# A chunked recurrence with two gated layers: the fills, the first keys and the first units of the start in another order

## The chip, the core and the metric

The kernel runs on one core of a Trainium2 chip. The metric is device time in microseconds (us), the median of several runs of one launch. The engines are named as in the profile: PE is TensorE's matrix multiply, PEld its weight load, DVE VectorE, ACT ScalarE, POOL GpSimd, SP the engine that issues the DMAs.

## The reference

Three layers follow one another. The first is a recurrence over 768 steps for 4 x 8 independent heads, with a state of 40 x 40:

```python
for t in range(S):
    y[:, :, t] = np.einsum('bhd,bhde->bhe', rt, state)
    Sa = np.einsum('bhde,bhe->bhd', state, at)
    state = state * wt[:, :, None, :] - np.einsum('bhd,bhe->bhde', Sa, bt) + np.einsum('bhd,bhe->bhde', vt, kt)
```

Its output, 3072 rows of 320, goes through `silu(x @ w_gate) * (x @ w_val) @ w_out` with 1536 hidden columns, and through a second such layer with `sigmoid` in place of `silu`. All data is float32.

## The kernel before, in words

**Chunks.** The 768 steps are cut into 12 chunks of 64. Inside a chunk the recurrence becomes matrix products and the inverse of one triangular 64 x 64 matrix per head pair (16 of them, `NS`). For each chunk `m` four generators do the work:

- `prep_a(m)` (line 435) scales the inputs a, b, k by running products of w, transposes them on PE (`tr4`, line 352) and forms the products `kps` ("keys", line 471). ACT negates them into `bn` (lines 480, 481), DVE masks them into `lq` (line 483).
- `prep_b(m)` (line 607) inverts. For chunks 0 to 2 `halves` (line 531) solves 16 x 16 blocks on DVE and joins them on PE; for the others `whole` (line 495) solves 32 x 32 blocks. Two more products, `zps` and `xps`, finish the inverse X; its last step is line 654 on ACT.
- `chain(m)` (line 657) carries the state `sT` from chunk to chunk: it copies the state into `Q` (line 667), transposes it into `sd` (lines 669, 670), and forms `qps`, `ups` (which needs X) and `sps`, for two halves of the heads. All three share one PSUM bank.
- `post(m)` (line 725) forms the chunk's outputs `ysb` (line 777).

**The running products of w.** Chunks 0 to 3 get them by a scan on DVE (line 138): chunk 0 in `first` (line 174), chunks 1 to 3 in `scanned` (line 388). The scan tiles of chunks 1 to 3 have the tags `raw3`, `raw4`, `raw5`, and the tile `one` that all scans read has the tag `raw2`. Chunks 4 to 11 get them from `powers(1)` and `powers(2)` (line 218): DVE clamps w (line 231), POOL multiplies (line 228, 29 products of 128 x 320 for a group), and the results go to DRAM (line 258) through two big tiles with the tags `wt` and `wq`.

**The gated layers.** `extra(m)` (line 1196) runs the first gated layer for the 128 x 2 rows of chunk `m`, with the weights loaded so far: `split` (transposes and a high and low part), then for each weight block 16 gate products (`gate`, line 976, tile `gv`) and 6 sums (`add`, line 994), which use the PSUM tags `po0` and `po1`. `extra(-2)` loads the first three weight blocks, `extra(0)` its own units and then blocks four and five. A weight block is loaded in three pieces (`load_w`, line 855): each goes from DRAM into a `raw` tile, through ACT (line 874), POOL (line 875), DVE (lines 878 to 884), ACT (line 894, the first write into the weight tile) and POOL (lines 896 to 902). The first three blocks use the tags `raw` and `raw1` by turns; from `extra(0)` on, all six from `raw` to `raw5` in turn, the fourth block beginning at `raw3`. Blocks four and five are stored in the tiles `wt` and `wq`, once `powers(2)` has let them go. The rest of the first layer and the second follow as one long stream on PE from about 700 us on.

**What sets the order.** Every loop step puts its generators into `merge` (line 790) with an interval and an offset, and `merge` emits the one whose next part is due first. The order of emission is a priority: a planner with a cost model of its own then places the instructions on each engine, and one that was emitted later can stand earlier where it is ready sooner. `behind` (line 111) pins an instruction behind a marked one of the same engine. Tiles with one tag share their memory, so a new one waits for every access to the one before. Each engine runs its list in order.

**Parts that the change touches.** `static` (line 58) collects the tiles that start as zero in `fills`; `fill` (line 80) lets ACT copy a zero into them. It is called at line 266 for `lq0` and at line 816, after `prep_a(0)`, for the other twelve. The marks are "keys" (the last product of `first` into `tkb`, line 199, for the first clamp of `powers(1)`), and "joined" and "merged" (the last products of chunk 0 at lines 586 and 642), behind which the first and third group of chunk 1's key transposes are pinned (line 465). `first` opens a PSUM pool of its own, whose banks go over to the pools of `banks()` afterwards; the two banks of `ptp`, which all transposes use, come first in it.

The start of the main loop reads:

```python
merge([(prep_a(0), 1, 0)])
fill()
...
merge(start)                     # prep_b(0) and prep_a(1)
for m in range(NCH + 1):         # cp(m), prep_b(m + 1), prep_a(m + 2), ahead(m) = extra(m - 1)
```

## Time and profile before

| | us |
|---|---|
| median of three runs | 1339.35 |
| lowest and highest of them | 1336.72, 1343.93 |
| the profiled execution | 1336.38 |
| its span, first to last instruction | 1334.6 |
| busy in it: PE, PEld, DVE, ACT, POOL | 1239.4, 1179.4, 754.5, 599.3, 563.1 |

All the times of the trace are of the profiled execution and count from the start of its span. A row of a timeline gives start and duration in us, engine, line, operation, the tile written and the one read, the shape, and in brackets the idle time of the engine just before it and what ended that. PEclk is the granted TensorE clock as a share of full speed. Chunk `m` is known by its place in the list of a line: the third L539 is that of chunk 2.

### The profile page before, as it was taken

What the parts mean: (1) busy time and instruction counts of PE and PEld (TensorE: products, weight loads), DVE (VectorE), ACT (ScalarE), POOL (GpSimd) and SP (SyncE); (2) the same over time, 40 slices, a digit from 0 to 9 for tenths busy, and PEclk for the clock granted to TensorE, in tenths of its full rate; (3) what the DMA queues carried; (4) which work ended last, traced back from release to release, by engine and by line L of the source; (5) the groups of instructions that cost most, each with busy time, mean ns of one, the idle gap of its engine ahead of it and who ended that gap; (6) DMA issues with size and microseconds to landing.
All of it is one profiled execution on the core that took longest, in us unless ns stands there. A gap on an engine that the chain in (4) does not pass through costs nothing.

```text
span 1334.6 us, 34566 instructions
## 1 busy us (share of the span) xinstructions
PE 1239.4 (93%) x14209; PEld 1179.4 (88%) x14209; DVE 754.5 (57%) x1578; ACT 599.3 (45%) x1446; POOL 563.1 (42%) x767
## 2 busy tenths in 40 slices
PE   5486889999999999989899999999999999999996
PEld 4475788898899888988898999999999999999995
DVE  6858667876687668775879888733122122211221
ACT  8353664556655565545444444423333333333331
POOL 5658241222322222445777888833222222222221
PEclk7667696999999999989999999999999999999998
DMA  7545823535533443253355555321000000000000
GB/s 211 125 123 131 191 91 103 124 98 129 144 92 99 129 123 90 70 139 102 118 172 179 190 167 165 97 81 56 23 23 23 23 23 23 23 23 23 11 11 14
DMA packets 153065, 126.16 MB, mean 95 GB/s; under 512 B 100928, under 2 KB 131136, under 8 KB 152640
## 3 DMA queue, kind: packets, MB, share of 16 engines
q1 hardware_dynamic: 152896, 123.84, 33.0%
q8 instruction: 114, 1.87, 0.6%
q14 instruction: 55, 0.45, 0.1%
HBM read 92.05 MB, written 31.76 MB: 93 GB/s over the span
## 4 chain that ended last, share of the span: by engine, by line
PE 75%; DVE 12%; issue 3%; ACT 3%; DMA 2%; POOL 2%; SPq 1%; POOLq 0%; DVEq 0%; ACTq 0%
PE g L976 30%; PE po L994 18%; PE gv L976 9%; PE tp L356 3%; PE kps L471 3%; PE aps L741 2%; PE yps L767 2%; PE qps L677 1%; PE ups L695 1%; SPq L258 1%; DVE dt L879 1%; DVE pr L511 1%; DVE part L517 1%; PE zps L626 1%; PE xps L642 1%
## 5 line engine op out<-in xcount | busy, mean ns | idle before, releaser
L976 PE MATMUL g<-x,w 128*128 128x256 f32 x3520 | 491.2, 283 | 4.1 <-DVE g L982 2.3
L976 PEld LDWEIGHTS g<-x,w 128*128 128x128 f32 x3520 | 460.5, 190 | 5.9 <-DVE g L982 3.2
L985 POOL TENSOR_TENSOR hl<-g,hh 128x256 fp32r<-128x256 f32 x288 | 218.9, 761 | 482.7 <-ACT hh L984 435.9
L983 DVE TENSOR_TENSOR g<-g,g 128x256 f32<-128x256 f32 x220 | 93.0, 423 | 308.7 <-PE g L976 299.1
L984 ACT CAST hh<-g 128x256 fp32r<-128x256 f32 x288 | 117.0, 406 | 259.7 <-DVE g L983 234.0
L994 PE MATMUL po<-w,hh 128*128 128x320 f32 x1152 | 225.3, 311 | 0.9 <-ACT hh L984 0.8
L994 PEld LDWEIGHTS po<-w,hh 128*128 128x128 f32 x1152 | 175.4, 189 | 2.2 <-ACT hh L984 1.7
L976 PE MATMUL gv<-x,w 128*128 128x256 f32 x1088 | 160.0, 296 | 5.9 <-ACT x L928 3.6
L976 PEld LDWEIGHTS gv<-x,w 128*128 128x128 f32 x1088 | 142.0, 197 | 11.9 <-ACT x L928 6.0
L980 ACT ACTIVATE g<-g 128x256 f32<-128x256 f32 x220 | 84.4, 384 | 132.4 <-PE g L976 120.7
L994 PE MATMUL po<-w,hl 128*128 128x320 f32 x576 | 141.9, 316 | 0.5 <-POOL hl L985 0.5
L896 POOL TENSOR_TENSOR dt<-dt,w 128x384 f32<-128x384 f32 (+1 forms) x72 | 78.5, 1091 | 72.4 <-ACT w L894 37.5
L994 PEld LDWEIGHTS po<-w,hl 128*128 128x128 f32 x576 | 91.9, 190 | 1.8 <-POOL hl L985 1.0
L483 DVE TENSOR_TENSOR lq<-kps,part 64x256 f32<-64x256 f32 x96 | 40.4, 421 | 86.5 <-ACT bn L481 82.8
L511 DVE TENSOR_TENSOR pr<-part,sn 128x4 f32<-128x4 f32 (+4 forms) x135 | 74.2, 550 | 2.9
L741 PE MATMUL aps<-rbd,ut 104*128 104x128 f32 x384 | 58.2, 295 | 14.1 <-DVE am L749 5.6
L517 DVE TENSOR_REDUCE part<-pr 128x2 f32<-128x4 f32 (+4 forms) x135 | 66.7, 494 | 3.1
L471 PE MATMUL kps<-lq,kbt 104*128 104x128 f32 x384 | 64.4, 320 | 3.4 <-ACT kbt L467 1.8
L356 PE MATMUL tp<-ident,part 128*104 128x128 f32 x288 | 50.0, 301 | 16.2 <-ACT pend L168 6.3
L741 PEld LDWEIGHTS aps<-rbd,ut 104*128 104x128 f32 x384 | 51.3, 203 | 15.6 <-issue 8.6
L471 PEld LDWEIGHTS kps<-lq,kbt 104*128 104x128 f32 x384 | 56.6, 226 | 7.2 <-issue 3.7
L894 ACT CAST w<-dt 128x384 fp32r<-128x384 f32 (+1 forms) x72 | 35.6, 494 | 57.1 <-DVE dt L879 49.1
(171 smaller groups left out, 1758.1 us busy)
## 6 DMA issues: line engine op xcount, KB each, us to landing
raw<-in_w_dram SPq DMA_DIRECT2D x48, 384.0 KB
xd<-x SPq DMA_DIRECT2D x12, 896.0 KB
x<-xd SPq DMA_DIRECT2D x12, 896.0 KB
raw<-in_w_dram SPq DMA_DIRECT2D x24, 320.0 KB
ld<-in_a_kb_dram SPq DMA_DIRECT2D x22, 320.0 KB
ld<-rd SPq DMA_DIRECT2D x32, 160.0 KB
pn<-pd SPq DMA_DIRECT2D x32, 160.0 KB
ld<-in_a_a_dram SPq DMA_DIRECT2D x12, 320.0 KB
```

The costliest lines, as they stand in the source:

```text
L356: t = nc.tensor.transpose(ps[0 : x.shape[1], n, :], x, ident)
L471: nc.tensor.matmul(kps[:, n].rearrange("p h t -> p (h t)"), lhsT=kbt[0:PW, n, :], rhs=lq[m % 3][0:PW, 4 * g4 + n].rearrange("p h t -> p (h ...
L511: nc.vector.tensor_tensor(out=o, in0=xs[:, 0:kk, None, 0:n].to_broadcast([P, kk, 2, n]), in1=sn[:, None, n : n + 2, 0:n].to_broadcast([P, ...
L517: nc.vector.tensor_reduce(out=xs[:, 0:kk, n : n + 2], in_=o, axis=AX.X, op=ALU.add)
L741: nc.tensor.matmul(aps[:, n, h2], lhsT=ut[0:PW, x, 2 * h2 : 2 * h2 + 2].rearrange("p u s -> p (u s)"), rhs=rbd[0:PW, x, h2].rearrange("p b ...
L896: sub(out=tf, in0=tf, in1=w.bitcast(F32), op=ALU.subtract)
L976: nc.tensor.matmul(gv[n], lhsT=p, rhs=q, start=e == 0, stop=e == len(seq) - 1)
L980: nc.scalar.activation(out=g, in_=gv[0], func=AF.Sigmoid)
L983: nc.vector.tensor_tensor(out=g, in0=gv[1], in1=g, op=ALU.mult)
L984: nc.scalar.copy(out=hh, in_=g)
L985: self.heng.tensor_tensor(out=hl, in0=g, in1=hh.bitcast(F32), op=ALU.subtract)
L994: self.nc.tensor.matmul(ops[u], lhsT=p[:, us], rhs=q, start=first and n == 0, stop=last and n == 2)
```

## The change

1. `fills` becomes a table by name. Five tiles (`lq0`, `qv`, `lq1`, `sT`, `x16`) are filled before `prep_a(0)`; the other eight after it, each pinned on ACT behind the mark "keys", which is now the last negation of the keys (line 481) emitted so far.
2. `first` puts a dummy tile over the first two banks of its PSUM pool, so that its own tiles lie in others. The small product and copy that make chunk 0's pending scale (lines 166 to 168) move from the end of `first` behind the transposes of `an` in `prep_a(0)`, into a tile of `ptp`. The banks of chunk 0's third and fourth key group change places.
3. Both clamps of `powers(1)` are pinned behind the last scaling of chunk 0's solve (line 569) instead of the first one behind the first keys.
4. The marks "joined" and "merged" go, and chunk 1's keys use three banks by turns instead of one.
5. In `halves` the sign scaling (line 540) and the diagonal (line 546) go from ACT to DVE.
6. For chunk 0 `chain` leaves out the copies of the state and its transposes, as the state is zero.
7. `extra(0)` is emitted at the end of loop step 0 instead of within step 1, ahead of `prep_a(3)` and `prep_b(2)`.

The diff without its plain renamings:

```diff
-    def fill():
-        for t in fills:
-            nc.scalar.copy(out=t, in_=zero[(slice(None),) + (None,) * (len(t.shape) - 2)].to_broadcast(t.shape))
-        fills.clear()
+    def fill(ts, mark=None):
+        for t in ts:
+            to = nc.scalar.copy(out=t, in_=zero[(slice(None),) + (None,) * (len(t.shape) - 2)].to_broadcast(t.shape))
+            if mark:
+                behind(to, mark)
...
-                marks.pop(name).ins.name,
+                marks[name].ins.name,
...
+            pp.tile([P, 2, 512], F32, tag="f", name="f")
             ps = [pp.tile([P, 10, 64 * i + 64], F32, tag=f"f{i}", name=f"f{i}") for i in range(2)]
...
-            pt = pp.tile([P, NS], F32, tag="f2", name="f2")
...
-            ends_scan(0, p, pt)
+            end_rows(p)
...
-            behind(clamp, "keys")
+            if n == 1:
+                behind(clamp, ("solved", 0))
...
-    lq = [static([P, NS, 2, C], "lq0", 0.0)]
-    fill()
+    lq = [static([P, NS, 2, C], f"lq{i}", 0.0) for i in range(3)]
...
-    fills.append(x16)
-    lq += [static([P, NS, 2, C], f"lq{i}") for i in (1, 2)]
     xinv = [static([P, NS, C], f"xinv{i}", part="part1") for i in range(2)]
-    fills.extend(lq[1:])
+    early = ("lq0", "qv", "lq1", "sT")
+    fill([fills[n] for n in early] + [x16])
...
+        if m == 0:
+            ends_scan(0, ptp.tile([P, 4, P], F32, tag="tp", name="pep")[:, 0, 0:NS])
...
-            ps = tr4(lambda n: tk[:, 4 * g4 + n], ("joined", None, "merged", None)[g4] if m == 1 else None)
+            ps = tr4(lambda n: tk[:, 4 * g4 + n])
...
-            pool, tag = ((pmm, "mm"), (pzy, "zy"), (pqu, "qu"), (po, "po1"))[g4 if m == 0 else 0]
+            pool, tag = ((pmm, "mm"), (pzy, "zy"), (po, "po1"), (pqu, "qu"))[g4 if m == 0 else g4 % 3 if m == 1 else 0]
...
-                nc.scalar.mul(out=bn[hi, q, 0:32], in_=kps[hi, :, h2, 32:64], mul=-1.0)
+                marks["keys"] = nc.scalar.mul(out=bn[hi, q, 0:32], in_=kps[hi, :, h2, 32:64], mul=-1.0)
...
-        nc.scalar.mul(out=sn, in_=full[:, :, 0:16], mul=par[:, 0:1])
+        nc.vector.tensor_scalar(out=sn, in0=full[:, :, 0:16], scalar1=par[:, 0:1], scalar2=None, op0=ALU.mult)
...
-        nc.scalar.mul(out=x16.rearrange("p r t -> p (r t)")[:, 1:256:34], in_=nk, mul=-1.0)
+        nc.vector.tensor_scalar(
+            out=x16.rearrange("p r t -> p (r t)")[:, 1:256:34], in0=nk, scalar1=-1.0, scalar2=None, op0=ALU.mult
+        )
...
-            nc.vector.tensor_scalar(out=to(0), in0=src, scalar1=sel[:, z : z + 1], scalar2=None, op0=ALU.mult)
+            marks[("solved", m)] = nc.vector.tensor_scalar(out=to(0), in0=src, scalar1=sel[:, z : z + 1], scalar2=None, op0=ALU.mult)
...
-        if m == 0:
-            marks["joined"] = last
...
-        if m == 0:
-            marks["merged"] = last
...
-            for h2 in range(2):
-                nc.scalar.copy(out=two(Q[E40[h2], h2, sg]), in_=pairs(sT, s4)[E40[h2]])
-
-            ps = tr4(lambda n: sT[:, 4 * hb + n])
-            nc.scalar.copy(
-                out=sd[0:PW, s4], in_=ps[0:PW].rearrange("p n (h e) -> p n h e", h=2)[..., 0:D]
-            )
+            if m:
+                for h2 in range(2):
+                    nc.scalar.copy(out=two(Q[E40[h2], h2, sg]), in_=pairs(sT, s4)[E40[h2]])
+
+                ps = tr4(lambda n: sT[:, 4 * hb + n])
+                nc.scalar.copy(
+                    out=sd[0:PW, s4], in_=ps[0:PW].rearrange("p n (h e) -> p n h e", h=2)[..., 0:D]
+                )
...
-    fill()
+    fill([t for n, t in fills.items() if n not in early], "keys")
...
-        todo.append((ahead(m), *(NX if m > 0 else QX)))
+        if m == 0:
+            todo.append((extra(0, out), 0.05, 3))
+        if m > 1:
+            todo.append((ahead(m), *NX))
```

## Rows read from the trace of the kernel before

**Rows 1.** The page: the chain of waits that ended last, by engine.
```profile
PE 75%; DVE 12%; issue 3%; ACT 3%; DMA 2%; POOL 2%; SPq 1%; POOLq 0%; DVEq 0%; ACTq 0%
```

**Rows 2.** Busy time by stretch: PE, PEld, DVE, ACT, POOL busy, PEclk, DMA share, GB/s.
```profile
0.00:40.00 40.00, 24.49 (x252) 21.86 (x252) 27.67 (x58) 31.50 (x54) 23.82 (x41) 0.79 0.64 176
40.00:60.00 20.00, 4.07 (x136) 3.13 (x136) 19.55 (x41) 6.38 (x13) 14.20 (x19) 0.54 0.68 156
60.00:160.00 100.00, 76.26 (x1359) 66.92 (x1360) 64.25 (x130) 47.32 (x110) 55.60 (x68) 0.67 0.65 145
160.00:260.00 100.00, 94.52 (x1494) 86.53 (x1494) 74.02 (x154) 55.24 (x131) 32.79 (x47) 0.82 0.37 108
```

**Rows 3.** Timeline of PE, 0 to 20 us: start, duration, line, tile, [idle before].
```profile
6.91 2.40 PE L153 MATMUL f<-ident,bn 128*64 128x64 f32 x40 [6.91 <-DVE bn L138]
...
18.82 1.95 PE L356 MATMUL tp<-ident,part 128*104 128x128 f32 x8 [6.27 <-ACT pend L168]
```

**Rows 4.** ACT: the fills' line (ns min/median/max, first and last start), then its timeline.
```profile
L82 ACT COPY part<-part x7: 534/719/1252, 3.9 to 11.6; 128x640 f32<-128x640 f32 x2, 128x416 f32<-128x416 f32 x2, 128x1280 f32<-128x1280 f32 x1, 128x832 f32<-128x832 f32 x1
L82 ACT COPY lq<-part x3: 1892/1892/1897, 2.1 to 14.2; 128x2048 f32<-128x2048 f32 x3
...
16.10 1.87 ACT L667 COPY part<-part 40x320 f32<-40x320 f32 x4
18.00 0.69 ACT L203 COPY pn<-f 128x640 f32<-128x640 f32 x1
```

**Rows 5.** Timelines of DVE and PE, 44 to 85 us: chunk 1's inputs and keys.
```profile
44.95 0.45 DVE L410 TENSOR_TENSOR tkb<-ld,dtp 128x128 f32<-128x128 f32 x2
...
55.51 1.90 PE L573 MATMUL hps<-x1t,bn 16*32 16x16 f32 x128 [8.89 <-DVE x1t L563]
...
61.42 1.95 PE L356 MATMUL tp<-ident,tkb 128*104 128x128 f32 x8
...
83.81 1.16 PE L471 MATMUL kps<-lq,kbt 104*128 104x128 f32 x8
```

**Rows 6.** Timeline of ACT: the last step of the inverses of chunks 0, 1, 3.
```profile
71.80 1.20 ACT L654 ACTIVATE part<-xps 32x512 f32<-32x512 f32 x2
...
149.63 1.20 ACT L654 ACTIVATE part<-xps 32x512 f32<-32x512 f32 x2
...
255.48 1.19 ACT L654 ACTIVATE part<-xps 32x512 f32<-32x512 f32 x2 [0.84 <-PE xps L642]
```

**Rows 7.** DVE: first and last step of two solves; products of L552 in each.
```profile
37.86 1.08 DVE L539 STREAM_TRANSPOSE sn<-bn 128x512 f32<-128x512 f32 x1
...
56.58 1.23 DVE L569 TENSOR_SCALAR part<-pr,part 128x256 f32<-128x256 f32 x2
...
149.98 1.02 DVE L539 STREAM_TRANSPOSE sn<-bn 128x512 f32<-128x512 f32 x1
...
161.92 1.76 DVE L569 TENSOR_SCALAR part<-pr,part 128x256 f32<-128x256 f32 x2
...
L552 DVE TENSOR_TENSOR pr<-x,sn x7: 297/625/1215, 45.9 to 52.9; 128x8 f32<-128x8 f32 x1, 128x32 f32<-128x32 f32 x1, 128x72 f32<-128x72 f32 x1, 128x128 f32<-128x128 f32 x1
...
L552 DVE TENSOR_TENSOR pr<-x,sn x7: 168/291/562, 153.1 to 157.8; 128x8 f32<-128x8 f32 x1, 128x32 f32<-128x32 f32 x1, 128x72 f32<-128x72 f32 x1, 128x128 f32<-128x128 f32 x1
```

**Rows 8.** Powers on POOL (10 to 80 us), chunk 0's scan, fourth weight's first write.
```profile
L228 POOL TENSOR_TENSOR wp<-wp x14: 849/864/2162, 17.4 to 52.6; 128x320 f32<-128x320 f32 x14
...
7.05 1.63 DVE L138 TENSOR_TENSOR_SCAN pr<-sn,one 128x264 f32<-128x264 f32 x3
...
139.20 0.51 ACT L894 CAST w<-dt 128x384 fp32r<-128x384 f32 x1 [3.67 <-issue]
```

**Rows 9.** Busy time of line 976 alone: PE, PEld, PEclk, DMA share, GB/s.
```profile
158.00:187.00 29.00, 8.45 (x48) 7.54 (x48) 0.83 0.37 118
```

**Rows 10.** Timelines of DVE and ACT: chunk 4's long solve and inverse.
```profile
238.51 1.23 DVE L497 STREAM_TRANSPOSE sn<-bn 128x1024 f32<-128x1024 f32 x1
...
296.97 1.19 ACT L654 ACTIVATE part<-xps 32x512 f32<-32x512 f32 x2 [1.92 <-PE xps L642]
```

More of the change, by code (lines that the diff above doesn't have):

```diff
@@ L53, in attention @@
     dr = ctx.enter_context(tc.tile_pool(name="at_dram", bufs=2, space=DRAM))
-    room, fills = {}, []
+    room, fills = {}, {}
     def static(shape, name, val=None, part=None):
@@ L74, in static @@
         if val == 0.0:
-            fills.append(t)
+            fills[name] = t
         elif val is not None:
@@ L157, in load_w0, with end_rows @@
         nc.sync.dma_start(out=x[:, :, 1 : C + 1], in_=w0[m].rearrange("p (j t) -> p j t", t=C))
-    def ends_scan(m, p, ps):
+    def end_rows(p):
         nc.vector.tensor_tensor(
@@ L165, in ends_scan @@
         )
+    def ends_scan(m, ps):
         nc.tensor.matmul(ps[0:PW], lhsT=pe[:, 0], rhs=hot, start=True, stop=True)
@@ L198, in first @@
                 sl = slice(8 * n, 8 * n + 8)
-                marks["keys"] = nc.vector.tensor_tensor(
+                nc.vector.tensor_tensor(
                     out=pairs(tkb[0], sl), in0=heads(xk)[:, sl], in1=ipv[:, sl], op=ALU.mult
@@ L350, in loads_late, with tr4 @@
             dma(out=ut[e, :, 1:3].rearrange("d n h t -> d n (h t)"), in_=vt[m, b2].rearrange("d (n t) -> d n t", t=P))
-    def tr4(get, name=None):
+    def tr4(get):
         ps = ptp.tile([P, 4, P], F32, tag="tp", name="tp")
@@ L355, in tr4 @@
             x = get(n)
-            t = nc.tensor.transpose(ps[0 : x.shape[1], n, :], x, ident)
-            if n == 0 and name:
-                behind(t, name)
+            nc.tensor.transpose(ps[0 : x.shape[1], n, :], x, ident)
         return ps
@@ L428, in scanned @@
                     turn(ps[:, 256 + 64 * i : 320 + 64 * i], p[:, 8 + i, 0:C], True)
-                ends_scan(m, p, ps[:, 384:400])
+                end_rows(p)
+                ends_scan(m, ps[:, 384:400])
                 by_p(ps[:, 256:384], slice(32, 40))
@@ L585, in halves @@
                 at = 32 * (j % 2) + 16
-                last = nc.tensor.matmul(
+                nc.tensor.matmul(
                     ps[32 * j : 32 * j + 16, q, 16:32],
@@ L641, in prep_b @@
                 lo, hi = slice(64 * h2, 64 * h2 + 32), slice(64 * h2 + 32, 64 * h2 + 64)
-                last = nc.tensor.matmul(
+                nc.tensor.matmul(
                     ps[lo, q],
```

## The prediction

> **What bounds the kernel now.** I read the chain of waits first. It gives TensorE three quarters of the span and VectorE an eighth [rows 1], so the end of the kernel moves only if TensorE gets its work earlier or has less of it. The busy time by stretch says where that can be [rows 2]. TensorE is busy for 94.5 of the 100 us from 160 to 260. Before 160 it is busy for 24.5 + 4.1 + 76.3 = 105 us, and most of that at a granted clock of 0.54 to 0.79. Weighted by the clock, the first 160 us hold 24.5 x 0.79 + 4.1 x 0.54 + 76.3 x 0.67 = 73 us of full-speed work, so 87 us are lost there. The next 100 us lose 100 - 94.5 x 0.82 = 22. Every part of the change lies in this start, so I looked for what TensorE waits for in it.
>
> There are three such places. From 12.6 to 18.8 it waits for ScalarE [rows 3]: the first transposes need a PSUM bank that `first` still holds. The row names the copy of the pending scale (L168), which stands right behind the copy that empties this bank (L203); L203 was ready at 9.3, when the transposes into it end [rows 3], but stands at 18.0 behind the fills and the copies of the zero state [rows 4]. From 46.6 to 55.5 it waits for VectorE, which solves chunk 0's triangular systems [rows 5], although the keys of chunk 1 were nearly ready: their transposes are pinned behind two marks of chunk 0 and start at 61.4, and the last product ends at 85.0 [rows 5]. And the inverse of each early chunk comes just in time or late: X is complete at 73.0, 150.8 and, for chunk 3, 256.7 [rows 6]; the chain of that chunk cannot start its second product earlier.
>
> **The change, part by part.**
>
> *Fills.* ScalarE's fills and zero-state copies run from 2.1 to 18.0 [rows 4]. With only five fills in front, two of 1.9 us and three of 0.4 to 1.25 [rows 4], some 6 us after the table load, the copy at L203 can run when its input is there, and the two PSUM banks put aside in `first` free the transposes of it. They then wait only for their own input and for the second scan's transposes. I take the whole wait, 6 us [rows 3]; the ends are 0 (the planner finds other work for ScalarE) and 9 (18.0 - 9.3). The eight late fills, three of 1.9 us and five of 0.5 to 0.6, still cost some 8 us on ScalarE after the first keys; the solve of chunk 0, which no longer uses ScalarE, covers them. Without that cover they would hold up chunk 1's copies by as much.
>
> *Clamps behind the solve, two ScalarE steps on VectorE.* The power products on GpSimd started at 17.4 [rows 8], behind a clamp on VectorE; now both clamps of the first group wait for chunk 0's solve. The solve took from 37.9 to 57.8, 20 us, with GpSimd multiplying beside it. Chunk 2's, with GpSimd idle for most of it, took 150.0 to 163.7, 13.7 us [rows 7]. The seven products of the solve show why: median 625 ns in the first case, 291 in the second [rows 7]. I take 7 us off the solve; the ends are 2 (weight conversion keeps GpSimd busy) and 9. The sign scaling and the diagonal move from ScalarE to VectorE: the nearest rows on VectorE, two pairs of scalings of 128x256, take 1.23 and 1.76 us a pair [rows 7], 0.6 to 0.9 each, about what a step and the hand-over to ScalarE take. So this is between 1 us gained and 1 us lost per chunk, and I count it in the 7.
> The Trainium skill (SBUF — State Buffer, Who interferes with whom) says that a VectorE instruction with two SBUF inputs, or one in a two-port mode, and a reading GpSimd instruction shut each other out. By that rule the contention is not removed but moves to chunk 1's solve, and the sum below would be 12 instead of 19, or 1327; the trace agrees with the rule on the products [rows 7]. I don't take it off: GpSimd was busy for 56 of the 100 us in which chunk 1's solve ran before [rows 2], so that solve paid already.
>
> *Keys of chunk 1.* Without the marks they may fill the 8.9 us gap [rows 5]. With three banks in place of one, a product no longer waits until the one before is read out. They need chunk 1's scaled inputs, ready at 45.4 [rows 5], so I put their end at about 68 instead of 85.
>
> *The zero state.* Four ScalarE copies of 0.46 us [rows 4], two more and eight transposes go: 3 us of TensorE and ScalarE at most, hidden in gaps. I give it nothing.
>
> *First units with chunk 0.* The 48 gate products and their sums move from 158 to 187, where TensorE is full, to the gaps before 150; the gate products alone are 8.5 us [rows 9]. They need chunk 1's inverse only for a PSUM bank.
>
> Together: the inverse of chunk 0 at about 57 (16 us earlier: 6 + 7, and 3 for the interleaved transposes), that of chunk 1 at about 105 instead of 151 (keys end at 68, then a solve and its five short products, as long as chunk 0's 73.0 - 37.9 = 35 us [rows 6, 7]). Chunks 0 to 2 and the first units are then through some 30 to 45 us earlier than before.
>
> **What is late next.** This does not all reach the end. Two power groups still have to run before the fourth and fifth weights can be written, as these use the same two tiles. And since the first units are now emitted with chunk 0, the pieces of the fourth weight claim the three raw tiles before the scan of chunk 3 does, which uses the same ones. So chunk 3's scan waits for the weight, and the weight for the second power group. Before, the first write of the fourth weight was released at 139.2 [rows 8]. The first product moves from 17.4 to about 47, behind a solve that ends near 45, which shifts this by 30 if all is rigid: 169. But GpSimd needed 36 us from the first to the last of 14 products of 0.86 us [rows 8], because the other products and the weight conversion stood between; with most of the conversion done before, 15 to 30 us of the shift come back. I take 150, ends 137 and 169. From there: 15 us for three pieces, then scan to inverse. For chunk 0 that was 8.7 to 73.0, 64 us [rows 6, 8]; chunk 3 has the long solve, which in chunk 4 took 59.7 us against 35, at low priority [rows 6, 10], so 0 to 25 more, and I take 12. The inverse of chunk 3 comes at 150 + 15 + 64 + 12 = 241, against 256.7: 16 us earlier (ends: 216, 41 earlier; 273, 16 later). TensorE has the second units and later keys to do in the meantime; I count 3 us for work it gets out of the way. **Sum: -19 us** on the profiled execution, whose own time is 1336.4 with a span of 1334.6. That is 1317; the median of the three runs is 3 above that execution, so I say 1320.
>
> **Rivals.** *The wait swallows it (19%).* If the fourth weight is released after about 160, chunk 3's inverse lands within 6 us of where it was, and the early gain is spent in TensorE waiting between chunks 2 and 3: 1333 to 1345. This also covers a planner that puts the new order back much as it was. For it: the planner's placing by priority, and a VectorE busy for 74 of 100 us from 160 to 260 [rows 2]. Against it: work that TensorE did meanwhile stays done.
> *Slower: the raw tiles (15%).* If all of the 30 us shift stays and the long solve takes its full 60, chunk 3's inverse comes at 169 + 15 + 64 + 25 = 273, 16 us late, and each later chunk is solved behind it: 1339 + 16 - 3 = 1352. The point from which it decides is a release after 169. For it: both power groups are serial through one pair of tiles, with a load and two stores between. Against it: GpSimd is idle for 44 of the 100 us from 60 to 160 [rows 2], room for the second group.
> *The clock follows (10%, inside the faster share).* The granted clock was 0.54 from 40 to 60, while TensorE was busy for a fifth of the time, and 0.67 in the 100 us after [rows 2]. With the gaps filled, the 76 us of work there could go at the upper level, 2.4 GHz, from the beginning: 76 x (1 - 0.67) = 25 us less, of which chunk 3's wait leaves perhaps half; 1320 - 13 = 1307. The Trainium skill (TensorE: Matmul & The Clock Gate, What's actually happening) says that the throttled state is the default and that activity releases it; by that rule this case is the expected one. I give it no more, since TensorE was busy for three quarters of that stretch and still had 0.67 [rows 2].
>
> **How the numbers follow.** The forecast, a gain of 8 to 30 us, has 56%; with the clock's 10% that is 0.66 for faster by over 0.5% (6.7 us, about what a measurement of this kernel can tell from no change). The swallowed gain has 19%, slower 15%. The range goes from 1339 - 41 = 1298, the early end of chunk 3's inverse, to 1345, the end of the swallowed case; of the slower case most lies outside.
>
> **What would show it.** First transposes at 12 to 14 with no wait on the copy for the pending scale; chunk 0's solve under 15 us; keys of chunk 1 in the gap at 45 to 65; the first gate products before 130 instead of 158.9; the fourth weight's first write near 150, and chunk 3's scan behind it. The forecast is wrong if chunk 1's inverse is not before 125, or if chunk 3's is not before 250.

## The result and the profile after

The changed kernel takes 1347.62 us (median of 14 runs, 1344.01 to 1350.24), the kernel before 1339.28 beside it: a ratio of 1.006, 95% interval [1.0047, 1.0073]. It is 8.3 us slower, where 19 us faster was predicted. The rival "slower: the raw tiles", with its 1352, comes near it.

The chain of waits of the changed kernel, by engine, stands against [rows 1]:

```profile
PE 68%; DVE 15%; DMA 5%; ACT 5%; issue 3%; POOL 3%; SPq 1%; DVEq 0%; POOLq 0%; ACTq 0%
```

TensorE's share of the chain falls from 75% to 68%, and other engines and transfers take it. The busy time by stretch says where (columns and stretches as in [rows 2]):

```profile
0.00:40.00 40.00, 25.14 (x252) 22.40 (x252) 24.93 (x60) 25.56 (x43) 10.72 (x30) 0.79 0.55 170
40.00:60.00 20.00, 11.69 (x296) 9.45 (x296) 17.68 (x41) 12.29 (x25) 9.63 (x10) 0.65 0.52 156
60.00:160.00 100.00, 71.53 (x1156) 62.53 (x1156) 66.10 (x124) 42.76 (x97) 67.66 (x88) 0.66 0.52 123
160.00:260.00 100.00, 79.12 (x1226) 70.95 (x1228) 64.31 (x135) 48.32 (x116) 30.37 (x38) 0.76 0.42 117
```

Weighted by the clock, TensorE does 25.14 x 0.79 + 11.69 x 0.65 + 71.53 x 0.66 = 75 us of full-speed work before 160, 2 more than before. From 160 to 260 it does 79.12 x 0.76 = 60, where it did 94.52 x 0.82 = 78 [rows 2]. So the start gained next to nothing, and 17 us went in the stretch that had been nearly full; the kernel is 8.3 us longer in the end.

What TensorE waits for in that stretch (timelines of ACT, DVE and PE, rows in order of time):

```profile
157.14 0.51 ACT L899 CAST w<-dt 128x384 fp32r<-128x384 f32 x1 [2.03 <-DMA pd<-wp]
...
165.10 2.13 DVE L139 TENSOR_TENSOR_SCAN s<-s,one 128x660 f32<-128x660 f32 x1
167.29 1.97 PE L154 MATMUL dtp<-ident,s 128*64 128x64 f32 x32 [3.71 <-DVE s L139]
171.72 2.00 DVE L139 TENSOR_TENSOR_SCAN s<-s,one 128x660 f32<-128x660 f32 x1
173.77 4.96 PE L154 MATMUL dtp<-ident,s 128*64 128x128 f32 x48 [4.52 <-DVE s L139]
186.15 0.55 DVE L719 TENSOR_TENSOR part<-part,pend 104x320 f32<-104x320 f32 x1
```

The first row is the first write of the fourth weight, 139.2 before [rows 8]; it waited for the store of the second power group (`pd`). Then chunk 3's two scans, and TensorE waits for them twice. The last row completes the first half of chunk 1's state. The same two scans, the state, and the last step of chunk 2's inverse in the kernel before:

```profile
115.23 1.58 DVE L138 TENSOR_TENSOR_SCAN s<-s,one 128x660 f32<-128x660 f32 x1
120.60 2.00 DVE L138 TENSOR_TENSOR_SCAN s<-s,one 128x660 f32<-128x660 f32 x1
...
166.15 0.49 DVE L717 TENSOR_TENSOR part<-part,pend 104x320 f32<-104x320 f32 x1
...
212.78 1.20 ACT L654 ACTIVATE part<-xps 32x512 f32<-32x512 f32 x2 [1.27 <-PE xps L642]
```

The scans come 50 us later than before, and the state 20.

The inverses of chunks 0 to 3 (ACT, last step, as in [rows 6]):

```profile
71.86 1.20 ACT L655 ACTIVATE part<-xps 32x512 f32<-32x512 f32 x2
...
139.55 1.20 ACT L655 ACTIVATE part<-xps 32x512 f32<-32x512 f32 x2
...
226.32 1.20 ACT L655 ACTIVATE part<-xps 32x512 f32<-32x512 f32 x2 [1.27 <-PE xps L645]
...
271.58 1.18 ACT L655 ACTIVATE part<-xps 32x512 f32<-32x512 f32 x2
```

Chunk 0's stayed where it was, chunk 1's came 10 us earlier, chunk 2's 14 and chunk 3's 16 later. The step from chunk 1's to chunk 2's grew from 63 to 87 us: there the gain turned into the loss.

### The profile page after: what moved, and what is told of

Read it like the earlier page. It is cut to its first block, busy times and chain, and to the rows that moved or that the text cites. A ratio compares the mean times of both kernels' runs of the same rounds, so it can differ in the third digit from the quotient of the medians.

```text
span 1347.7 us, 34551 instructions
## 1 busy us (share of the span) xinstructions
PE 1242.2 (92%) x14201; PEld 1177.9 (87%) x14201; DVE 759.4 (56%) x1584; ACT 594.5 (44%) x1434; POOL 559.7 (42%) x767
## 4 chain that ended last, share of the span: by engine, by line
PE 68%; DVE 15%; DMA 5%; ACT 5%; issue 3%; POOL 3%; SPq 1%; DVEq 0%; POOLq 0%; ACTq 0%
PE g L981 26%; PE po L999 16%; PE gv L981 8%; PE tp L358 3%; PE aps L743 3%; PE kps L474 2%; PE yps L769 2%; PE qps L679 2%; DVE dt L884 1%; DVE ds L889 1%; DVE pr L514 1%; PE ups L697 1%; DVE part L520 1%; DMA wt<-in_a_w_dram 1%; DVE g L987 1%
## 5 line engine op out<-in xcount | busy, mean ns | idle before, releaser
L889 DVE SCALAR_TENSOR_TENSOR ds<-raw,ds 128x384 f32<-128x384 uint32 (+1 forms) x72 | 60.0, 833 | 1.2
```

## Experiments

Eighteen kernels were timed against the kernel before, each beside runs of its own of that kernel. The medians can differ from the ratios by some tenths of a per cent, so effects are given by the ratios, in points (1 point is 1%, 13.4 us). The times of the inverses and of chunk 3's first scan (us) are the starts of these steps in one trace of each.

| kernel | us | ratio and 95% interval | inverse of 1, 2, 3 | scan of 3 |
|---|---|---|---|---|
| before | 1339.28 | | 150, 213, 255 | 115 |
| changed | 1347.62 | 1.006 [1.0047, 1.0073] | 140, 226, 272 | 165 |
| A: without 7 | 1335.69 | 1.0003 [0.9979, 1.0027] | 149, 211, 256 | 110 |
| B: loads late | 1333.08 | 0.9969 [0.9949, 0.9989] | 151, 215, 260 | 113 |
| C: without 3 | 1351.7 | 1.0113 [1.0092, 1.0133] | 161, 228, 271 | 143 |
| D: 7 alone | 1332.67 | 0.9967 [0.9944, 0.999] | 136, 204, 247 | 147 |
| E: without 3, 7 | 1326.1 | 0.9892 [0.9859, 0.9924] | 136, 204, 249 | 111 |
| F: B, pieces held | 1334.98 | 0.998 [0.995, 1.0009] | 148, 214, 255 | 121 |
| G: keys of 3 later | 1352.46 | 1.0102 [1.008, 1.0125] | 138, 214, 265 | 166 |
| H: B, keys of 2 later | 1349.82 | 1.0077 [1.0051, 1.0104] | 131, 225, 270 | 129 |
| I: B without 3 | 1338.1 | 0.9982 [0.995, 1.0013] | 139, 205, 251 | 113 |
| J: E without 4 | 1344.46 | 1.0044 [1.0021, 1.0067] | 161, 225, 268 | 122 |
| K: E without 1, 2 | 1344.88 | 1.0043 [1.0023, 1.0063] | 139, 211, 256 | 120 |
| L: E without 5 | 1331.39 | 0.9942 [0.9922, 0.9962] | 138, 204, 249 | 121 |
| M: A, second clamps later | 1329.23 | 0.9928 [0.9907, 0.995] | 140, 205, 253 | 113 |
| N: changed, two raw tiles | 1335.67 | 0.9996 [0.997, 1.0023] | 137, 204, 250 | 117 |
| O: E, pieces held | 1341.98 | 1.0034 [1.0013, 1.0055] | 155, 218, 259 | 123 |
| P: C, two raw tiles | 1321.49 | 0.9865 [0.9832, 0.9897] | 138, 203, 249 | 112 |
| Q: changed, M's and N's edits | 1327.4 | 0.9926 [0.9898, 0.9954] | 138, 211, 256 | 114 |
| R: D, two raw tiles | 1336.88 | 0.9994 [0.9974, 1.0015] | 150, 218, 265 | 115 |

### Undoing parts 7 and 3 (A to D)

A puts the first units back into step 1. B leaves them with chunk 0 and moves only the loading of the fourth and fifth weight back into step 1. C takes part 3 out (only the first clamp of the first group is pinned, behind chunk 0's scaled keys). D is the kernel before with part 7 alone.

```diff
 A
-        if m == 0:
-            todo.append((extra(0, out), 0.05, 3))
-        if m > 1:
-            todo.append((ahead(m), *NX))
+        todo.append((ahead(m), *(NX if m > 0 else QX)))
 B
-                for f in {-2: range(NFA - 2), 0: range(NFA - 2, NFA)}.get(m, ()):
+                for f in {-2: range(NFA - 2), -3: range(NFA - 2, NFA)}.get(m, ()):
...
+        if m == 1:
+            todo.append((extra(-3, out), NX[0], NX[1] + 6 * NX[0]))
 C
-            if n == 1:
-                behind(clamp, ("solved", 0))
+            if n == 1 and i == 0:
+                behind(clamp, "scaled")
```

Theory A in these expectations is the claim of the scan tiles, B the late power products, C the early units standing in chunk 1's way.

> The changed kernel with extra(0), units and weights four and five, back in loop step 1. Theory A (the pieces of the fourth weight claim the scan tiles of chunk 3, so its scan waits until 165 and its transposes hold both transpose banks while chunk 1's state waits for one): the scan of chunk 3 falls back to 75 to 125, the state of chunk 1's first half is updated before 160 instead of 186, and the time is 1318 to 1335, below both kernels. Theory B (the late power products themselves cost the time, through the weights and GpSimd): chunk 3's scan is early but the time stays at 1343 to 1349. Theory C (the early units crowd out chunk 1): the scan moves, and the time falls to about 1339, the kernel before.

> The changed kernel with the units of extra(0) still in loop step 0, but the loads of weights four and five back in step 1, behind chunk 3's scan. Theory A: as good as the run with both back, within 4 us, or up to 10 us better, since the units then fill gaps: 1315 to 1335. Theory B: 1343 to 1349. Theory C: the units alone cost it, so 1343 to 1349 as well, but with chunk 3's scan before 125.

> The changed kernel with the clamps of the first power group as before: the first one behind chunk 0's scaled keys, near 16 us, not behind the solve. Theory B: powers start 35 us earlier, the fourth weight is written before 130, chunk 3's scan comes before 140 and the time is 1320 to 1338. Theory A: partly so, since the claim on the tiles stays but ends earlier: 1330 to 1343. Theory C: no change, 1344 to 1350.

> The kernel before with nothing but extra(0), units and loads, moved into loop step 0. Theory A: chunk 3's scan moves from 115 to behind the fourth weight's first write, which stays near 139, so to about 147 to 155; the time is 1343 to 1352. Theory B: the powers are where they were, so no more than 2 us: 1337 to 1342. Theory C: 1345 to 1350.

A and B take 0.6 and 0.9 points off the changed kernel, and chunk 3's scan is back at 110 and 113. A alone does not decide: it is level with the kernel before, as theory C had it, just outside theory A's range, and chunk 1's state came at 169.6 and not before 160. In B, which lies in theory A's range, the early units are still in, so it is the weights' loading that costs. C lies outside all three ranges, and the wrong way: the weight was released early (132), yet the kernel is slower still. So undoing the late power products alone brings nothing back; what they cost is read from E and A below. D is outside all three too: its scan came at 147, the inverses early, and it is a little faster than before.

### The claim on the scan tiles by itself (N, P, R)

The pieces of the fourth and fifth weight are emitted as in the change, but go through the two raw tiles of the first three, and so claim none of the scan's. Nothing else is edited.

```diff
-                if m == 0:
+                if m == 1:
                     ffn.raw = raws
```

> The changed kernel, all parts in, emitted in the same order; only the pieces of the fourth and fifth weight go through the two raw tiles that the first three used, so that they claim none of the three scan tiles. Theory A (the loss is chunk 3's scan waiting for those tiles): scan of chunk 3 at 105 to 125 instead of 165, step from chunk 1's to chunk 2's inverse 62 to 70 us instead of 87, 1328 to 1338. If the pieces' places in the queues of ScalarE, VectorE and GpSimd are what costs: 1343 to 1350.

Theory A is met: 0.64 points less than the changed kernel, which leaves N level with the kernel before. ACT, DVE and the inverses of chunks 1 to 3 of N, then its busy time from 160 to 260:

```profile
117.40 1.53 DVE L139 TENSOR_TENSOR_SCAN s<-s,one 128x660 f32<-128x660 f32 x1
124.31 1.66 DVE L139 TENSOR_TENSOR_SCAN s<-s,one 128x660 f32<-128x660 f32 x1
...
156.34 0.51 ACT L899 CAST w<-dt 128x384 fp32r<-128x384 f32 x1
...
136.74 1.20 ACT L655 ACTIVATE part<-xps 32x512 f32<-32x512 f32 x2
...
204.22 1.20 ACT L655 ACTIVATE part<-xps 32x512 f32<-32x512 f32 x2 [0.43 <-PE xps L645]
...
249.98 1.19 ACT L655 ACTIVATE part<-xps 32x512 f32<-32x512 f32 x2 [0.86 <-PE xps L645]
```

```profile
160.00:260.00 100.00, 91.84 (x1487) 82.18 (x1486) 79.50 (x159) 56.09 (x134) 33.41 (x46) 0.80 0.54 135
```

The weight's first write is where the change has it (156 against 157). The scan moved, by 48 us, and with it the step between the inverses of chunks 1 and 2, from 87 to 67. TensorE is busy for 92 us of this stretch again. So the loss is not the late weight itself, which is as late in N; it is chunk 3's scan standing behind it.

> The changed kernel with the clamps as before (1351.7), and the weight pieces through two raw tiles. Theory A in its second form (with early clamps the loss is the fourth weight's first cast, which stands on ScalarE for 9.9 us in front of the copies for chunk 2's keys, not the scan tiles): the cast still waits 5 us or more, chunk 1's inverse after 150, 1342 to 1352. If the scan tiles decide here too: scan of chunk 3 before 125 and 1326 to 1336.

P was expected to part the scan tiles from the cast on ScalarE, and doesn't quite; its time is 4.5 us below the lower of the two ranges. In C that cast does hold up an engine (ACT and PE of C):

```profile
132.39 0.51 ACT L899 CAST w<-dt 128x384 fp32r<-128x384 f32 x1 [9.92 <-DMA pd<-wp]
...
134.07 1.07 PE L358 MATMUL tp<-ident,tkb 128*104 128x128 f32 x4 [6.29 <-POOL dt L901]
```

ScalarE stood there for 9.9 us with the copies behind it that empty the transposes' banks (PE's row names another engine, but the next row of ACT is the copy at line 457). With two raw tiles the cast stands at 141.3 in P and doesn't wait at all, and the scan is at 112, so both causes went together. P has the lowest time of the study (E's interval overlaps with its own): with all parts but 3, and the weight pieces in two raw tiles, it takes 1.35% less than before.

> The kernel before with part 7 alone (1332.7), and the weight pieces through two raw tiles. There the scan of chunk 3 came at 147 instead of 115, and the time fell all the same. If a scan at 147 is not yet late (the step from chunk 1's to chunk 2's inverse was 67.7 us, as without a wait): 1329 to 1335, as with part 7 alone. If the scan already cost something there: 1320 to 1328.

R is no faster than D; it lies 2 us above the first range. A scan at 147 was not late in D, whose step from inverse 1 to 2 is 68 us, as in the kernels without a wait. The pair is not a clean one, though: in R the inverse of chunk 1 came 14 us later than in D, so more than the scan moved. A scan at 165 was late (N); from when on it is late is not shown. C, with 143, lost by another way.

### Is it what stands behind the scan on TensorE? (G)

In the changed kernel the transposes of chunk 3's scan stand on TensorE ahead of the keys and of chunk 1's state. G emits chunk 3's scan and keys later.

```diff
-            todo.append((prep_a(m + 2), *(NA if m else QD)))
+            todo.append((prep_a(m + 2), *(((0.1058, 0.6) if m == 1 else NA) if m else QD)))
```

> The changed kernel with the scan and keys of chunk 3 emitted later in step 1 (offset 0.6 instead of -0.4), the weights where the change has them. Theory A1 (the loss is TensorE standing in its order at chunk 3's scan transposes, with chunk 1's state behind them): chunk 1's state is transposed at 158 to 168 instead of 184 to 190, TensorE busier from 160 to 200 than 24 us, 1334 to 1341. Theory A2 (the loss is that chunk 3's inverse comes late, whatever stands in front): the inverse of chunk 3 at 272 or later, 1346 to 1356.

Chunk 1's state and two of chunk 3's key products in G (DVE, PE):

```profile
153.32 0.48 DVE L719 TENSOR_TENSOR part<-part,pend 104x320 f32<-104x320 f32 x1
...
188.63 1.06 PE L474 MATMUL kps<-lq,kbt 104*128 104x128 f32 x8
...
215.21 2.08 PE L474 MATMUL kps<-lq,kbt 104*128 104x128 f32 x8 [0.18 <-ACT part L655]
```

The state is complete at 153.8 instead of 186.7, and chunk 2's inverse 12 us earlier, but chunk 3's keys now end at 217 and its inverse stays late, at 265. The time is 0.4 points worse than the changed kernel's (a part of that can be the fall of the clock that the last section describes). A2 is met by the time, though not by its mark of 272: as far as these two kernels show, the order on TensorE decides which chunk pays for the late scan.

### What part 3 costs (E, M, Q)

E is A and C together: parts 1, 2, 4, 5 and 6 alone. It shows that the rest of the change is worth 1.1%. M is A with the second power group's clamps pinned behind chunk 2's last scaled keys; Q is the changed kernel with M's and N's edits.

```diff
-            if n == 1:
-                behind(clamp, ("solved", 0))
+            behind(clamp, ("solved", 0) if n == 1 else ("scaled", 2))
```

> The changed kernel without parts 3 and 7 (clamps as before, first units in step 1). With part 7 undone alone it took 1335.7. Theory P (the late clamps cost something of their own: they push the second power group to 111 to 121 us, where VectorE's queue waits for its load and chunk 2's keys stand behind): 1326 to 1331, second clamps near 88, chunk 2's keys before 125. Rival Q (the late clamps help by freeing chunk 0's solve from GpSimd): 1336 to 1343, chunk 0's solve 18 us or more instead of 15.

> The changed kernel without part 7 (1335.7), with the second power group's clamps pinned on VectorE behind the last scaling of chunk 2's keys. Without part 3 as well it took 1326.1, so part 3 costs 9.6. Theory P1 (the cost is VectorE standing for 5 us at the second clamp, whose load comes at 117, with chunk 2's scaled inputs and TensorE's transposes behind it): chunk 2's transposes start 4 to 6 us earlier than 118.5, chunk 1's inverse before 145, 1326 to 1331. Theory P2 (the cost lies in the powers being late themselves, whatever stands behind the clamp): 1334 to 1341.

> The changed kernel with all seven parts and both mends: weight pieces through two raw tiles (alone 12 us less than the changed kernel), second group's clamps behind chunk 2's scaled keys (alone 6.5 us less). If the two losses are separate, they add: 1326 to 1332, scan of chunk 3 before 125, chunk 2's transposes before 118. If late power products cost something beside the wait at the clamp, more than the 1321.5 of the kernel with early clamps and two raw tiles; if the two losses share one wait: 1334 to 1340.

P is met in E, at the lower end of its range, with the second clamps at 89.5; but chunk 2's keys end at 147 there and not before 125. P1 is met in M by the time and by chunk 1's inverse. A first, then M (DVE and PE, around 117 us):

```profile
116.72 1.49 DVE L234 TENSOR_SCALAR wp<-wq 128x2560 f32<-128x2560 f32 x1 [5.08 <-DMA wq<-in_a_w_dram]
118.13 0.28 DVE L403 TENSOR_TENSOR part<-ld,dtp 128x128 f32<-128x128 f32 x1
118.47 1.09 PE L358 MATMUL tp<-ident,part 128*104 128x128 f32 x4 [5.58 <-DVE part L403]
```

```profile
114.67 0.26 DVE L402 TENSOR_TENSOR part<-ld,dtp 128x128 f32<-128x128 f32 x1
115.63 0.65 PE L357 MATMUL tp<-ident,part 128*104 128x128 f32 x4
...
120.85 1.50 DVE L234 TENSOR_SCALAR wp<-wq 128x2560 f32<-128x2560 f32 x1 [3.84 <-issue]
```

With part 3 the first power group ends late, so the load of the second comes late, and its clamp meets chunk 2's scaling in VectorE's queue: 5.1 us of VectorE and 5.6 us of TensorE. With the clamp behind, the transposes start at 115.6 (2.8 us earlier, where 4 to 6 were expected), and 0.75 of the 1.1 points that part 3 costs are back. Q adds this to N's gain as expected, but stays 0.6 points above P: late power products cost something beside this wait, and what that is was not found. One candidate stands in Q's trace: ScalarE waits 4.9 us there for the store in front of the fourth weight's first cast, at 155, and not at all in P; no run isolates it.

### Which of the other parts carries the gain (J, K, L)

J puts part 4 back as it was before (marks, one bank), K parts 1 and 2, L part 5, each in E.

```diff
 J
-            ps = tr4(lambda n: tk[:, 4 * g4 + n])
+            ps = tr4(lambda n: tk[:, 4 * g4 + n], ("joined", None, "merged", None)[g4] if m == 1 else None)
 K
-    fill([fills[n] for n in early] + [x16])
+    fills.extend(lq[1:])
...
-            pp.tile([P, 2, 512], F32, tag="f", name="f")
 L
-        nc.vector.tensor_scalar(out=sn, in0=full[:, :, 0:16], scalar1=par[:, 0:1], scalar2=None, op0=ALU.mult)
+        nc.scalar.mul(out=sn, in_=full[:, :, 0:16], mul=par[:, 0:1])
```

> The kernel without parts 3 and 7 (1326.1), with part 4 undone as well: chunk 1's keys pinned behind chunk 0's joining products and in one bank. If the gain of 13 us comes from chunk 1's earlier keys, this is within 4 us of before: 1335 to 1341, keys of chunk 1 ending near 90 and its inverse near 150. If it comes from fills or from ScalarE, 1326 to 1331.

> The kernel without parts 3 and 7 (1326.1), with parts 1 and 2 undone as well: all fills before the keys or en bloc after them without a mark, no dummy tile, the pending scale at the end of the first stage. The first transposes go back from 16 to 18.8. If these 3 us at the start go through to the end, 1329 to 1332; if the fills' place decides more (ScalarE free before the keys), 1334 to 1340; if the gain is that of the keys of chunk 1, 1326 to 1329.

> The kernel without parts 3 and 7 (1326.1), with part 5 undone as well: sign scaling and diagonal of the solve on ScalarE again. By the prediction's term, between 1 us gained and 1 us lost per chunk in the three solves, hidden or not: 1324 to 1330. If ScalarE's queue held those solves up (its late fills stand in front of them), 1331 to 1338 and chunk 0's solve ending after 62.

No one part carries it. Without part 4, chunk 1's inverse comes at 161, later than before the change (150), and the kernel is slower than before by 0.4%, more than its case had it. Without parts 1 and 2 it loses as much, though the first transposes are only 0.9 us later than in E (16.9 against 16.0) and chunk 1's keys end earlier, at 61.7; that is more than any of the three cases had it, and the trace does not settle where it goes. Part 5 is worth some 0.5 points there, more than its term: chunk 0's solve takes 25 us in L and 20.6 in E. It ends at 61.5 in L, next to the mark of the second case, in whose range the time lies.

### Weight pieces, chunk 2's keys, early units (F, H, I, O)

F and O pin the fifth and later weight pieces on ScalarE behind chunk 0's inverse; H gives chunk 2's scan and keys the offset 0.5 for -1; I is B with C's edit, that is E with early units and late loads.

```diff
 F, O
+    def held():
+        for i, _ in enumerate(extra(-2, out)):
+            if i > 3:
+                behind(first_of["piece"], ("inverse", 0))
+            yield
...
-            todo.append((extra(-2, out), *QW))
+            todo.append((held(), *QW))
 H
-    QD = (0.0971, -1)
+    QD = (0.0971, 0.5)
```

> Based on the changed kernel with the fourth and fifth weight loaded in step 1 (1333.1); in addition the fifth and later weight pieces stand on ScalarE behind chunk 0's inverse. Theory D (chunk 0's inverse stayed at 73 because ScalarE stood at the piece at 62 us, whose tile waits for GpSimd's power products): the inverse completes at 65 to 69. Whether the end follows: if early inverses of chunk 0 set the end, 1326 to 1329; if the next chunk's inverse does, which comes 60 us after its solve, 1331 to 1336.

> The kernel without parts 3 and 7 (1326.1), with the fifth and later weight pieces pinned on ScalarE behind chunk 0's inverse. If chunk 0's inverse (76 there) is on the path: inverse at 68 to 71, 1319 to 1323. If chunk 1's inverse follows its own queue, as with the pieces held in the other kernel: chunk 1's inverse stays at 134 to 138, 1324 to 1330.

> Based on the changed kernel with the fourth and fifth weight loaded in step 1 (1333.1); the scan and keys of chunk 2 are emitted later in step 0 (offset 0.5 instead of -1). Theory E (chunk 1's inverse came 60 us after its solve since its joining products stand on TensorE between chunk 2's scan transposes): chunk 1's inverse completes at 105 to 125 instead of 152. If that is what the early chunks wait for: 1316 to 1326. If the gain is spent on waiting for chunk 2 or 3: 1330 to 1340.

> The changed kernel with the clamps as before and the first units with chunk 0, but the fourth and fifth weight loaded in step 1; that is the kernel without parts 3 and 7 (1326.1) plus early units. If the loss of part 7 lies in the weight pieces alone (they claim the scan tiles, and their first cast stands on ScalarE before chunk 2's keys), the units by themselves cost nothing: 1320 to 1328, first cast of the fourth weight after 140 with under 2 us of waiting on ScalarE, chunk 3's scan near 112. If the units themselves are in the way: 1334 to 1345.

Chunk 0's inverse does come forward in F, by 6 us to 67.7, and the end doesn't follow: chunk 1's stays at 148. In O it comes at 73, later than either case had it, and the pieces that return after it (the last at 130 instead of 115) push chunk 1's inverse back by 18 us. H's theory was right in kind (chunk 1's inverse 20 us earlier, though not in the range) and no use, as chunk 2's came 11 us later. I is C with late loads and 1.3 points faster than C, as B is faster than the changed kernel; but it is 0.9 points slower than E, and lies in the range of "the units in the way". P, which has the same units early, is not slower than E, which speaks against that. The one trace of I has a fall of the clock that the last section shows; if its other runs have it too, that is about half of the 0.9. The rest is open.

## Why the prediction was wrong, step by step

**The step that failed** is "what is late next", in the term from chunk 3's scan to its inverse: 64 + 12 = 76 us were taken, and it took 99. The wait itself was foreseen, place and resource. The fourth weight was to be released at 150 (ends 137 and 169) and came at 157, inside. The first power product had moved by 35 us (from 17.4 to 52.7, where I had 30), and GpSimd recovered 17 of them, within the 15 to 30 expected. The pieces took 16.6 us, from the release at 157.1 to the end of the second scan at 173.7, where I took 15. The next marks are chunk 3's last key products and the first step of its long solve (PE and DVE of the changed kernel):

```profile
206.02 1.06 PE L474 MATMUL kps<-lq,kbt 104*128 104x128 f32 x8
...
210.33 1.23 DVE L500 STREAM_TRANSPOSE sn<-bn 128x1024 f32<-128x1024 f32 x1
```

From the scan to this solve it is 36.6 us; chunk 0, the model, took 29. From there to the end of the inverse at 272.8 it is 62.4, where 35 + 12 = 47 were taken. So the sum was 24 us short, and 15 of them lie in the long solve and its join. The rows had the right size for it: 59.7 for chunk 4 [rows 10], and chunk 3's own had taken 71 before (185.5 to 256.7). Another 7 lie between scan and solve. There the scan's transposes and the keys stand in one queue on TensorE with chunk 1's state, and putting that first did not bring chunk 3's keys earlier (G).

The size of the end was off as well: by the forecast's own count an inverse 16 us late is worth 13 us, and 8.3 were measured; R, whose inverse of chunk 3 comes 9 us late, is level with the kernel before.

The rival "slower: the raw tiles" had the right cause and the right inverse (273 against 272.8), the latter by luck: it counted 104 us from a release at 169, and it was 115.6 from 157. Its price was 13 against 8.3, and its point of decision, "a release after 169", was wrong. N shows the claim by itself to be worth 0.64 points. Both marks set for a wrong forecast were passed: chunk 1's inverse at 140 and not before 125, chunk 3's at 272 and not before 250.

**Fills.** The first transposes moved from 18.8 to 15.6 and not to 12.6; 3 of the 6 us came. PE's row for them:

```profile
15.64 1.92 PE L358 MATMUL tp<-ident,part 128*104 128x128 f32 x8 [2.82 <-DVE tkb L202]
```

The wait is now for VectorE's last scaling of chunk 0's keys, the last reader of the first stage's banks: the dummy tile did not make two banks free on their own, as far as this row tells (a kernel with the fills and without the tile was not tried). In K, which keeps all fills in front, the transposes start at 16.9, and the copy that empties their bank at 16.1 instead of 18.0: 1.9 of the 3.2 us are the four zero-state copies gone from ScalarE, to which I had given nothing.

**Clamps and solve.** Chunk 0's solve went from 20 us to 15.3, where I took 13 (DVE, first and last step):

```profile
35.87 1.05 DVE L542 STREAM_TRANSPOSE sn<-bn 128x512 f32<-128x512 f32 x1
...
50.39 0.79 DVE L574 TENSOR_SCALAR part<-pr,part 128x256 f32<-128x256 f32 x2
```

In E, with the clamps early and part 5 in, it takes 20.6 again. So that mechanism is right and its size was 4.7, not 7. By the Trainium skill (SBUF — State Buffer, Who interferes with whom) a VectorE instruction with two SBUF inputs and a GpSimd instruction that reads SBUF shut each other out. By that rule the contention would move to chunk 1's solve. The trace agrees only in part: the seven products fall from 625 to 347 ns on average in chunk 0's solve, but in chunk 1's they take 537, against 555 before, so nothing was added there. What I did not price is the other end of part 3: the second group's load and clamp moved to 111 and 119, in front of chunk 2's scaling on VectorE. That costs more than the shorter solve brings: 1.1 points, A against E, all told.

**Keys of chunk 1** ended at 73.3, forecast 68, before 85.0: 12 of the 17 us came.

**The inverses of chunks 0 and 1** were forecast for 57 and 105, and came at 73.1 and 140.8; this was the second error. Chunk 0's, in POOL, ACT and PE order:

```profile
52.66 4.85 POOL L231 TENSOR_TENSOR wp<-wp 128x320 f32<-128x320 f32 x3 [3.80 <-DVE wp L234]
...
62.03 0.56 ACT L879 ACTIVATE dt<-raw 128x384 f32<-128x384 f32 x1 [5.03 <-POOL w L905]
62.61 0.76 ACT L603 ACTIVATE part<-hps 16x256 f32<-16x256 f32 x2
63.43 1.92 PE L629 MATMUL zps<-x1t,bn 32*32 32x32 f32 x64 [5.42 <-ACT part L603]
```

The power products now begin just as the solve ends, and hold up a weight piece on GpSimd; ScalarE waits for that piece's tile with the copy for chunk 0's join behind it, and TensorE behind that. For chunk 1 the solve was done at 94.3, 21 us after its keys, as the model has it. But its joining products stood in pieces between chunk 2's scan transposes on TensorE (PE; first, last and next step):

```profile
92.17 0.60 PE L578 MATMUL hps<-x1t,bn 16*32 16x16 f32 x26
...
122.16 0.83 PE L578 MATMUL hps<-x1t,bn 16*32 16x16 f32 x46
...
127.19 0.35 PE L591 MATMUL hps<-part,pr 32*16 32x16 f32 x22
```

The second batch (line 591) started 35 us after the first, with chunk 2's late inputs between. I had used the length of chunk 0's solve and join for chunk 1, as if no other chunk were on the engines.

**First units.** The first gate products came at 138.8 instead of 158.9, not before 130. Alone, part 7 brings 0.3 points (D).

**The clock** did not follow: 0.66 from 60 to 160, against 0.67. Nor did that stretch become denser, with 71.5 us busy against 76.3 [rows 2]. In P, the fastest, it did (the two stretches from 60 and from 160):

```profile
60.00:160.00 100.00, 80.43 (x1336) 71.81 (x1328) 68.04 (x138) 46.59 (x108) 62.23 (x76) 0.62 0.60 146
160.00:260.00 100.00, 92.08 (x1541) 82.11 (x1541) 78.72 (x161) 57.77 (x138) 29.05 (x41) 0.88 0.42 123
```

TensorE is busy for 80 us of the first stretch and granted 0.62, less than before; the second gets 0.88 for 0.82. In M it is busy for 68 us of the first stretch and granted 0.69. By the Trainium skill (TensorE: Matmul & The Clock Gate, What's actually happening) activity releases the throttle. Taken over the whole of the first stretch, no run here shows that.

## What to carry to other kernels

When work is emitted earlier, list every tile tag that it claims, and ask who else needs these tiles next and from when on that one would be late: here a scan that was 30 us late in D at no visible cost was made 50 us late by a weight that nobody needed yet. Moving a chain of work later moves its loads too, and an instruction that waits for such a load can hold up what stands behind it in the queue of its engine, as A's clamp did for 5 us. A stage's length measured at the start, with little else running, was too short here for the same stage in company (29 against 36.6 us from scan to solve); where the trace has a nearer row, take that one.

## What the runs showed that had not been expected

**VectorE beside GpSimd.** One 128x384 operation took 3.87 us while GpSimd ran products of 128x320; the same line took 0.36 us a hundred us later (the changed kernel, DVE):

```profile
64.54 3.87 DVE L883 TENSOR_SCALAR dt<-dt 128x384 int32<-128x384 int32 x1
...
163.05 0.36 DVE L883 TENSOR_SCALAR dt<-dt 128x384 int32<-128x384 int32 x1 [1.75 <-POOL dt L880]
```

**A clock that falls late.** In the one trace of five of the eighteen kernels (B, D, H, I, K) the granted clock falls to 0.50, the 1.2 GHz level, for some 10 us between 290 and 330, with TensorE fully busy for most of it; in G, O and R it falls for a shorter time. I, by stretch (the columns of [rows 2]):

```profile
296.00:300.00 4.00, 3.11 (x42) 2.79 (x44) 2.07 (x2) 1.87 (x5) 0.08 (x1) 0.68 0.46 146
300.00:304.00 4.00, 4.00 (x46) 3.81 (x43) 1.62 (x3) 0.10 (x1) 1.68 (x2) 0.50 0.40 90
304.00:308.00 4.00, 4.00 (x41) 3.29 (x40) 2.25 (x4) 3.18 (x8) 0.00 (x0) 0.50 0.77 244
308.00:312.00 4.00, 4.00 (x46) 3.59 (x46) 0.85 (x2) 2.78 (x9) 0.00 (x0) 0.61 0.00 0
312.00:316.00 4.00, 4.00 (x34) 3.67 (x34) 1.98 (x5) 1.64 (x5) 0.00 (x0) 1.00 0.56 229
```

A wait of 1.9 us ended just before it, at 296.9. Here 3.11 x 0.32 + 8 x 0.50 + 4 x 0.39 = 6.6 us of full-speed work go with it. The kernel before has a wait of 2.4 us at the same place and its clock stays at 1.00, so the wait alone doesn't bring it about; what does was not found.

**Parts that don't add.** Part 7 was worth 0.3 points on the kernel before (D), and cost 0.6 on the other six parts (the changed kernel against A) and 2.2 on the other five without part 3 (C against E). With a planner that places every instruction anew, single parts taken one at a time say little here. The inverse of chunk 3 goes with the time at the ends only: the seven kernels that have it by 253 run from 0.9865 to 0.9996, and of the five with 264 or later beside the changed one (C, G, H, J, R) four are slower than before, while R is level with it. The six between, at 255 to 260 (A, B, F, K, O, Q), run from 0.9926 to 1.0043 in no such order, so that inverse does not set the end by itself.
